# The third pair's rows in a buffer of their own, loaded between words; the first word operations behind the second pair's Exp

## The chip, the cores and the metric

One core of a Trainium2 chip runs the whole program. The metric is device time in microseconds for one execution. Engines are named as in the profile: PE is TensorE, DVE VectorE, ACT ScalarE, POOL GpSimd, SP SyncE.

## The reference

Attention with RMS-normalised q and k over 4 batches of 12 heads (448 positions, 64 features), and then two MLPs on 1792 tokens of 768 features:

```python
def rmsnorm(x, g):
    rms = np.sqrt(np.mean(x * x, axis=-1, keepdims=True) + 1e-06)
    return x / rms * g
q_n, k_n = rmsnorm(q, g_q), rmsnorm(k, g_k)
scores = np.matmul(q_n, k_n.transpose(0, 1, 3, 2)) / np.sqrt(64)
attn = softmax(scores)            # over the last axis
x = concat_heads(attn @ v)        # 1792 x 768
h = x @ w_in                      # 768 x 2048
x = np.maximum(0.01 * h, h) @ w_out
a, b = x @ w1, x @ w2             # 768 x 1024 each
out = ((a * b) @ w3) @ w_out2     # 1024 x 1024, 1024 x 768
```

Weights are 64-bit numbers; q, k and v are float32.

## The kernel before

The last two products have nothing between them, so the kernel multiplies their weights together first (w3 with w_out2, which it calls w_last; `combine_weights`, TensorE's line L554 with tile `pw`), during the first heads of the attention. The rest is the attention itself, two heads (a pair) at a time, and the MLPs, for which every product is made of float32 parts, a high one and a low one: a row of three matmuls (high by high, high by low, low by high).

A weight tile that comes as 64-bit numbers is loaded as **words** (768 KB for a tile of w_last, 512 KB for one of w3) and turned into float32 (`raw`) by four steps, written `to_float32`: ScalarE works on the high words in place (L470) and VectorE shifts them into raw (L472); ScalarE works on the low words in place (L474) and VectorE adds them to raw (L476). Then the parts: for w_last, GpSimd makes lasth (L110) and lastl (L199); for w3, ScalarE makes wh (L505) and VectorE wl (L199). The first four tiles of w_last and the first of w3 (t from 0 to 4 in the list of weights) are asked for at the start through SyncE's queue; later ones through ScalarE's, each behind an operation of ScalarE on earlier words (`self.rounded`).

A **pair** t of heads takes this way: `load_rows(t)` loads q and k with a position's features in a row (two DMAs, `qk_sb`, L139), two buffers for all pairs in turn; `statistics(t)` squares them (ScalarE, L153), sums (VectorE, L154), takes ScalarE's Ln (L157) and Exp (L158) for 1 / rms, refines it by a Newton step of five small operations (L160 to L164, on GpSimd but for the first pair), and scales k (VectorE, L174: kn). `keys(t)` transposes kn (TensorE, `pk`, L220) and splits it in kh (ScalarE, L229) and kl (VectorE, L230); `scores` multiplies with qh and ql (TensorE, `ps`, L128), VectorE scales (`p`, L265) and ScalarE takes the Exp (L274); `p_transpose` turns p (TensorE, `pt`) for `values`, which multiplies with v (`load_v`).

Pairs 0 and 1 are loaded by name at the start, pair 2's rows and statistics in step 0 of the list of attention steps. A scheduler with a model of time puts each engine's instructions in one order, by priorities and by `issue_after` (an instruction, or a DMA, doesn't stand ahead of the given one). At run time each engine and each DMA queue goes through its own order, waiting at whatever isn't ready. The queues' completions are counted on eight **lanes**, dealt out in turn; a DMA that gets a lane waits until the lane's DMA before has landed.

## Time and profile before

| what | value |
| --- | --- |
| time of the kernel, median of 3 runs | 1178.95 us (1178.59 to 1179.77) |
| the profiled execution's own time | 1182.5 us |
| its span, first to last instruction | 1180.7 us |
| TensorE busy | 1137.4 us, 96% of the span |
| VectorE, ScalarE, GpSimd busy | 710.1, 657.7, 243.6 us |
| mean granted clock of TensorE | 0.987 of full |

The runs' times count the whole program on the device; the span is that of one profiled execution, and lies 1.8 us below that execution's own time. TensorE is busy nearly all the time, so the views that tell something are those of the stretches in which it isn't.

### The profile page before, as it was taken

To read this page: it belongs to the slowest core of one execution; us is meant where nothing else is said; L and a number is where in the kernel's file an instruction comes from. 1 tells how busy PE (TensorE), PEld (TensorE's weight loads), DVE (VectorE), ACT (ScalarE), POOL (GpSimd) and SP (SyncE) were. 2 spreads that over 40 slices of the span, in tenths; PEclk is the share of its full clock that TensorE was granted. 3 is DMA by queue.
4 is the path that set the end of the run, shared out by engine and by line. 5 is a ranking of instruction groups with operands and counts; after the bars stand their busy time and mean duration, and the time that the engine had idled before them with its cause. 6 is when DMAs were issued, how large, how long until landed. Compare 5 with 4: busy or idle time off the path is not lost.

```text
span 1180.7 us, 16739 instructions
## 1 busy us (share of the span) xinstructions
PE 1137.4 (96%) x6096; PEld 956.8 (81%) x6096; DVE 710.1 (60%) x1334; ACT 657.7 (56%) x1347; POOL 243.6 (21%) x345
## 2 busy tenths in 40 slices
PE   3899999999999999999999999999999999899998
PEld 2678867677787888888888888879999999699997
DVE  7986776877423667567545643483445556954553
ACT  6978687987534566676556643354443344443331
POOL 5632344544212232345222011000000000000000
PEclk8799999999999999999999999999999999999999
DMA  9556565985865446346332421440212212102112
GB/s 315 182 176 221 174 204 193 326 279 186 292 209 162 153 139 206 127 138 200 123 120 95 161 87 43 143 151 28 81 51 57 69 41 78 55 29 89 55 36 103
DMA packets 74979, 164.51 MB, mean 139 GB/s; under 512 B 13968, under 2 KB 42384, under 8 KB 74896
## 3 DMA queue, kind: packets, MB, share of 16 engines
q1 hardware_dynamic: 55392, 80.06, 22.5%
q10 hardware_dynamic: 10800, 48.76, 12.3%
q0 software_dynamic: 8704, 34.61, 7.8%
q8 instruction: 48, 0.79, 0.3%
q14 instruction: 35, 0.29, 0.1%
HBM read 120.46 MB, written 42.95 MB: 138 GB/s over the span
## 4 chain that ended last, share of the span: by engine, by line
PE 84%; DVE 7%; ACT 4%; DMA 3%; issue 1%; ACTq 0%; SPq 0%; POOL 0%; DVEq 0%; POOLq 0%
PE ps_mm L554 32%; PE ps_o L554 13%; PE ps_b L554 9%; PE pt L308 6%; PE ps L128 6%; PE po L128 6%; PE ps_c L554 5%; PE pw L554 5%; PE ps_a L554 2%; DVE ol L199 1%; DMA wh<-kept_first_mlp_h 1%; ACT p L274 1%; DVE wl L199 1%; PE pk L220 1%; ACT w L474 1%
## 5 line engine op out<-in xcount | busy, mean ns | idle before, releaser
L199 DVE TENSOR_TENSOR wl<-raw,wh 128x512 fp32r<-128x512 f32 (+1 forms) x136 | 109.4, 807 | 112.4 <-ACT wh L505 73.5
L265 DVE TENSOR_SCALAR_CACHE_REDUCE p<-ps,rs 112x448 f32<-112x448 f32 x192 | 122.2, 680 | 42.4 <-PE ps L128 42.4
L554 PE MATMUL ps_mm<-xl,wh 128*128 128x448 f32 x384 | 146.2, 381 | 0.0
L554 PE MATMUL ps_mm<-xh,wh 128*128 128x448 f32 x384 | 141.3, 368 | 2.3 <-DMA wh<-kept_first_mlp_h 2.3
L274 ACT ACTIVATE p<-p,low 112x448 f32<-112x448 f32 x192 | 126.5, 662 | 30.1 <-DVE p L265 29.8
L554 PE MATMUL ps_mm<-xh,wl 128*128 128x448 f32 x384 | 141.5, 368 | 0.7 <-DMA wl<-kept_first_mlp_l 0.7
L554 PE MATMUL ps_mm<-gl,wh 128*128 128x448 f32 x288 | 109.5, 381 | 0.0
L554 PE MATMUL ps_mm<-gh,wl 128*128 128x448 f32 x288 | 105.6, 367 | 1.6 <-DMA wl<-kept_first_mlp_l 1.6
L554 PE MATMUL ps_mm<-gh,wh 128*128 128x448 f32 x288 | 106.0, 369 | 1.1 <-DMA wh<-kept_first_mlp_h 1.0
L554 PE MATMUL ps_o<-gl,wh 128*128 128x448 f32 x288 | 104.3, 366 | 0.0
L554 PE MATMUL ps_o<-gh,wl 128*128 128x448 f32 x288 | 100.8, 366 | 0.0
L308 PEld LDWEIGHTS pt<-ident,p 112*112 112x112 f32 x768 | 82.2, 136 | 21.3 <-issue 7.1
L554 PE MATMUL ps_o<-gh,wh 128*128 128x448 f32 x288 | 99.4, 366 | 0.0
L470 ACT ACTIVATE w<-w 128x768 f32<-128x768 f32 (+1 forms) x80 | 63.4, 792 | 64.6 <-DMA w<-w_out 29.7
L308 PE MATMUL pt<-ident,p 112*112 112x112 f32 x768 | 96.2, 265 | 0.0
L505 ACT ACTIVATE wh<-raw 128x512 fp32r<-128x512 f32 (+1 forms) x84 | 59.2, 706 | 56.5 <-PE ps_mm L554 52.6
L554 PEld LDWEIGHTS ps_mm<-xl,wh 128*128 128x128 f32 x384 | 72.4, 189 | 12.5 <-issue 7.2
L476 DVE CUSTOM_DVE_ANT_0 raw<-w,raw 128x1024 uint16<-128x1024 uint16 (+1 forms) x80 | 79.2, 995 | 2.2 <-ACT w L474 0.5
L554 PEld LDWEIGHTS ps_mm<-xh,wh 128*128 128x128 f32 x384 | 72.3, 188 | 9.4 <-issue 3.7
L784 ACT ACTIVATE wh<-raw 128x512 fp32r<-128x512 f32 (+1 forms) x52 | 36.3, 698 | 76.3 <-PE ps_b L554 33.7
L554 PEld LDWEIGHTS ps_mm<-xh,wl 128*128 128x128 f32 x384 | 72.6, 189 | 7.6 <-issue 1.6
L128 PE MATMUL po<-pth,v_sb 112*64 112x448 f32 x384 | 77.5, 545 | 0.0
(141 smaller groups left out, 2530.5 us busy)
## 6 DMA issues: line engine op xcount, KB each, us to landing
w<-w_in ACTq DMA_DIRECT2D x16, 768.0 KB, 5.8
w<-w_out ACTq DMA_DIRECT2D x24, 512.0 KB, 3.9
w<-w ACTq DMA_DIRECT2D x16, 768.0 KB, 4.5
qk_sb<-qk SPq DMA_DIRECT2D x48, 224.0 KB, 4.0
w<-w3t ACTq DMA_DIRECT2D x15, 512.0 KB, 4.6
kept_first_mlp<-raw POOLq DMA_DIRECT2D x16, 384.0 KB, 4.3
kept_first_mlp<-raw POOLq DMA_DIRECT2D x24, 256.0 KB, 3.2
kept_second_mlp<-raw POOLq DMA_DIRECT2D x16, 384.0 KB, 2.9
```

The lines of the kernel that those rows point to most:

```text
L128: one = nc.tensor.matmul(out, a, x, start=begin, stop=end)
L199: e.tensor_tensor(out, x, y.bitcast(F32), op=ALU.subtract)
L220: nc.tensor.transpose(pk[:, c * CP : (c + 1) * CP], kn[:, c].rearrange("p h d -> p (h d)"), ident[:CP, :CP],)
L265: nc.vector.tensor_scalar(p, ps[c % 2][e], x["scale"][:, e, c : c + 1], None, op0=ALU.mult, op1=ALU.min, accum_out=low,)
L274: exps[t] = nc.scalar.activation(p, p, AF.Exp, bias=low, scale=-1.0, accum_out=x["sums"][:, e, c : c + 1])
L308: nc.tensor.transpose(pt[:, c * CP : (c + 1) * CP], h["p"][c][:, kc * CP : (kc + 1) * CP], ident[:CP, :CP],)
L470: nc.scalar.activation(h, h, AF.Prelu, scale=2.0**-112, alpha=2.0**32)
L474: self.rounded = nc.scalar.activation(low, low, AF.Copy, scale=2.0**-29)
L476: nc.vector.tensor_tensor(top, top, low, op=ALU.add)
L505: self.rounded = nc.scalar.activation(flat[0], x, AF.Copy)
L554: nc.tensor.matmul(ps[:, :n], a, x, start=begin, stop=end, skip_group_check=on)
L784: nc.scalar.activation(parts[0], x, AF.Copy)
```

## The change

Pair 2's rows get a pool `extra` of one buffer, so their load needn't wait for pair 0's buffer. They are asked for in `Weights.load` directly behind the words of tile 1, and the first v behind those of tile 3. The words of tiles 2 and 3 stand behind the last load issued up to there (`start["dma"]`) in place of the second pair's `qt`. Step 0 of the attention no longer asks for v or rows; pair 3 takes pair 0's buffer. ScalarE's operations on the words of tiles 0 to 4 stand behind the Exp of pair 1's 1 / rms (`start["words"]`); before, those of tiles 0 and 1 stood behind kh of pair 0 (`start["keys"]`), and the others behind nothing.

```diff
+    extra = early_words.enter_context(tc.tile_pool(name="extra", bufs=1, side="right"))
...
         b, j = divmod(2 * t, H)
-        x = pairs[t]["rows"] = io.tile([CP, 2, 2, NCH, D], F32, tag="qk", name="qk_sb", bufs=2)
+        if t == 2:
+            x = extra.tile([CP, 2, 2, NCH, D], F32, name="qk_sb")
+        else:
+            x = io.tile([CP, 2, 2, NCH, D], F32, tag="qk", name="qk_sb", bufs=2)
+        pairs[t]["rows"] = x
...
-        nc.scalar.activation(rs, y, AF.Exp, scale=-0.5)
+        start["roots"] = nc.scalar.activation(rs, y, AF.Exp, scale=-0.5)
...
                 else:
-                    load_v(2 * t)
                     ranked(prep, t + 1)
-                    load_rows(t + STATS_AHEAD)
+                    if t:
+                        load_v(2 * t)
+                        load_rows(t + STATS_AHEAD)
...
-            with tc.issue_after((self.rounded or start["ins"]).ins):
-                eng.dma_start(x[:, :n], src.rearrange("p (n t) -> p n t", t=2))
+            behind = self.rounded or start["dma" if t in (2, 3) else "ins"]
+            with tc.issue_after(behind.ins):
+                dma = eng.dma_start(x[:, :n], src.rearrange("p (n t) -> p n t", t=2))
+            with tc.issue_after(dma.ins):
+                if t == 1:
+                    load_rows(2)
+                elif t == 3:
+                    load_v(0)
...
-            with tc.issue_after(start["keys"].ins) if t < 2 else ExitStack():
+            with tc.issue_after(start["words"].ins) if t <= KH2 else ExitStack():
                 nc.scalar.activation(h, h, AF.Prelu, scale=2.0**-112, alpha=2.0**32)
...
+    start["words"] = start["roots"]
```

KH2 is 4. The line numbers of the changed kernel are higher by up to 13. How the order moves, at three places. Numbers behind names tell buffers apart; the changed kernel's are a little higher (pair 2's rows are qk_sb_292 before and qk_sb_299 after).

ScalarE, around the squares of pair 2's rows, before. What stands in brackets is what the instruction waits for, DMAHW followed by a digit being a lane:

```order
L153 ACTIVATE sq_370<-qk_sb_292 112x512 [waits DMAHW0_49]
L153 ACTIVATE qk_sb_292<-qk_sb_292 112x512 [waits DMAHW1_49]
L451 DMA w64_467<-w_last 128x1536 [waits DVE_49]
L451 DMA w64_478<-w_last 128x1536 [waits DVE_49]
L470 ACTIVATE w64_356<-w64_356 128x768 [waits DMAHW2_49]
L474 ACTIVATE w64_356<-w64_356 128x768
L505 ACTIVATE wh_480<-raw_473 128x512 [waits DVE_49]
L451 DMA w3_487<-w3t 128x1024
```

And in the changed kernel:

```order
L158 ACTIVATE sq_373<-qk_sb_299 112x512 [waits DMAHW2_49]
L158 ACTIVATE qk_sb_299<-qk_sb_299 112x512
L458 DMA w64_470<-w_last 128x1536 [waits DMAHW2_49,DVE_49]
L482 ACTIVATE w3_389<-w3_389 128x512 [waits DMAHW4_49]
L486 ACTIVATE w3_389<-w3_389 128x512
L458 DMA w64_481<-w_last 128x1536 [waits DVE_49]
L517 ACTIVATE wh_483<-raw_476 128x512 [waits DVE_49]
L458 DMA w3_490<-w3t 128x1024 [waits DMAHW5_49]
L458 DMA w3_561<-w3t 128x1024 [waits DMAHW6_49]
L107 ACTIVATE pth_395<-pt_396 112x448 [waits PE_49]
L482 ACTIVATE w64_359<-w64_359 128x768
L486 ACTIVATE w64_359<-w64_359 128x768
```

The fifth tile of w_last (w64_356 before, w64_359 now) has gone from ahead of wh to behind it and an eviction (pth); the second w3 tile's two steps stand ahead of wh in its place. The issue of w64_470 now waits for lane 2, which is the lane of pair 2's rows and, in turn, of the first half of pair 3's rows (qk_sb_503), the next DMA that SyncE puts on it.

VectorE, from the first p of pair 1's scores on, before:

```order
L265 TENSOR_SCALAR p_448,low_449<-ps_432,rs_142 112x448
L472 TENSOR_SCALAR raw_492<-w64_356 128x768
L265 TENSOR_SCALAR p_452,low_453<-ps_433,rs_142 112x448
L199 TENSOR_TENSOR wl_481<-raw_473,wh_480 128x512
L476 ISA raw_492<-w64_356,raw_492 128x1536
L472 TENSOR_SCALAR raw_529<-w3_386 128x512
L265 TENSOR_SCALAR p_456,low_457<-ps_434,rs_142 112x448
L265 TENSOR_SCALAR p_460,low_461<-ps_435,rs_142 112x448
L476 ISA raw_529<-w3_386,raw_529 128x1024
```

And in the changed kernel:

```order
L270 TENSOR_SCALAR p_451,low_452<-ps_435,rs_145 112x448
L270 TENSOR_SCALAR p_455,low_456<-ps_436,rs_145 112x448
L204 TENSOR_TENSOR wl_484<-raw_476,wh_483 128x512
L484 TENSOR_SCALAR raw_495<-w64_359 128x768
L484 TENSOR_SCALAR raw_532<-w3_389 128x512
L270 TENSOR_SCALAR p_459,low_460<-ps_437,rs_145 112x448
L270 TENSOR_SCALAR p_463,low_464<-ps_438,rs_145 112x448
L488 ISA raw_495<-w64_359,raw_495 128x1536
L488 ISA raw_532<-w3_389,raw_532 128x1024
```

The fifth w_last tile's second step (to raw_492 before, raw_495 now) has gone from behind wl to behind wl, both first steps and two p.

GpSimd, from the fourth tile's lastl on, before:

```order
L199 TENSOR_TENSOR lastl_156<-raw_429,lasth_155 128x768
L110 TENSOR_SCALAR lasth_155<-raw_492 128x768
L160 TENSOR_SCALAR ss_369<-ss_369 112x16
L199 TENSOR_TENSOR lastl_156<-raw_492,lasth_155 128x768
L161 TENSOR_TENSOR y_376<-rs_375 112x16
L162 TENSOR_TENSOR y_376<-y_376,ss_369 112x16
L163 TENSOR_SCALAR y_376<-y_376 112x16
L110 TENSOR_SCALAR lasth_155<-raw_579 128x768
L164 TENSOR_TENSOR rs_375<-y_376,rs_375 112x16
L199 TENSOR_TENSOR lastl_156<-raw_579,lasth_155 128x768
```

And in the changed kernel:

```order
L204 TENSOR_TENSOR lastl_159<-raw_432,lasth_158 128x768
L165 TENSOR_SCALAR ss_372<-ss_372 112x16
L111 TENSOR_SCALAR lasth_158<-raw_495 128x768
L204 TENSOR_TENSOR lastl_159<-raw_495,lasth_158 128x768
L166 TENSOR_TENSOR y_379<-rs_378 112x16
L167 TENSOR_TENSOR y_379<-y_379,ss_372 112x16
L168 TENSOR_SCALAR y_379<-y_379 112x16
L111 TENSOR_SCALAR lasth_158<-raw_582 128x768
L169 TENSOR_TENSOR rs_378<-y_379,rs_378 112x16
L204 TENSOR_TENSOR lastl_159<-raw_582,lasth_158 128x768
```

The first Newton operation of pair 2 (ss) now stands ahead of the fifth tile's lasth; the others stand behind its lastl as before. For pair 1, further up, all five stand together, where lasth and lastl of the first tile stood between them.

SyncE's queue: before, v, words 0, 4, 1, a qt, words 2 and 3, a v, a qt, pair 2's rows, pair 3's rows; now words 0, 4, 1, the first half of pair 2's rows, a qt, their second half, words 2 and 3, a qt, both v, pair 3's rows, pair 4's rows.

## Rows read from the trace of the kernel before

**Rows 1.** The page's head and its first part: busy time of TensorE.

```profile
span 1180.7 us, 16739 instructions
...
PE 1137.4 (96%) x6096; PEld 956.8 (81%) x6096; DVE 710.1 (60%) x1334; ACT 657.7 (56%) x1347; POOL 243.6 (21%) x345
```

**Rows 2.** Waits of TensorE from 0 to 120 us: total, times, longest.

```profile
PE pk L220 <- DVE qk_sb L174: 9.3, 1, 9.3
PE pk L220 <- ACT p L274: 5.8, 1, 5.8
PE ps L128 <- DVE kl L230: 3.8, 1, 3.8
PE pw L554 <- DVE wl L199: 2.2, 1, 2.2
PE pw L554 <- ACT wh L505: 1.9, 2, 1.6
```

**Rows 3.** Two windows: busy us and count of PE, PEld, DVE, ACT, POOL; clock, DMA share, GB/s.

```profile
25.00:30.00 5.00, 1.76 (x8) 0.83 (x8) 5.00 (x4) 1.60 (x5) 4.92 (x4) 0.82 1.06 320
50.00:55.00 5.00, 5.00 (x30) 4.25 (x29) 5.00 (x8) 5.00 (x12) 3.93 (x4) 0.93 0.00 0
```

**Rows 4.** Timeline of ScalarE, 10 to 50 us: start, duration, instruction, [idle before <-releaser].

```profile
25.82 0.19 ACT L274 ACTIVATION_READ_ACCUMULATOR p<-p,low 112x1 f32 x1
29.06 0.60 ACT L153 ACTIVATE sq<-qk_sb 112x512 f32<-112x512 f32 x1 [3.06 <-DMA qk_sb<-qk]
30.02 0.63 ACT L153 ACTIVATE qk_sb<-qk_sb 112x512 f32<-112x512 f32 x1 [0.36 <-DMA qk_sb<-qk]
...
30.89 0.92 ACT L470 ACTIVATE w<-w 128x768 f32<-128x768 f32 x1 [0.24 <-DVE r L284]
...
32.52 0.62 ACT L505 ACTIVATE wh<-raw 128x512 fp32r<-128x512 f32 x1
...
40.12 0.20 ACT L158 ACTIVATE rs<-y 112x16 f32<-112x16 f32 x1
```

**Rows 5.** Timeline of VectorE, 10 to 50 us, same columns.

```profile
20.75 0.69 DVE L174 TENSOR_TENSOR qk_sb<-qk_sb,rs 112x512 f32<-112x512 f32 x1
...
25.78 4.09 DVE L476 CUSTOM_DVE_ANT_0 raw<-w,raw 128x1536 uint16<-128x1536 uint16 x2
29.79 0.67 DVE L230 SCALAR_TENSOR_TENSOR kl<-pk,gqk,kh 128x448 fp32r<-128x448 f32 x1
...
34.70 0.95 DVE L476 CUSTOM_DVE_ANT_0 raw<-w,raw 128x1536 uint16<-128x1536 uint16 x1
35.56 0.42 DVE L472 TENSOR_SCALAR raw<-w 128x512 uint32<-128x512 uint32 x1
35.90 0.68 DVE L265 TENSOR_SCALAR_CACHE_REDUCE p<-ps,rs 112x448 f32<-112x448 f32 x1
...
37.11 2.32 DVE L476 CUSTOM_DVE_ANT_0 raw<-w,raw 128x1024 uint16<-128x1024 uint16 x1
...
43.90 2.32 DVE L174 TENSOR_TENSOR qk_sb<-qk_sb,rs 112x512 f32<-112x512 f32 x1 [1.67 <-POOL rs L164]
46.14 0.68 DVE L199 TENSOR_TENSOR wl<-raw,wh 128x512 fp32r<-128x512 f32 x1
```

**Rows 6.** Timeline of GpSimd, 10 to 50 us, same columns.

```profile
35.74 0.94 POOL L110 TENSOR_SCALAR lasth<-raw 128x768 fp32r<-128x768 f32 x1 [3.25 <-DVE raw L476]
...
37.03 1.84 POOL L199 TENSOR_TENSOR lastl<-raw,lasth 128x768 fp32r<-128x768 f32 x1
40.41 1.90 POOL L161 TENSOR_TENSOR y<-rs 112x16 f32<-112x16 f32 x1 [1.53 <-ACT rs L158]
42.38 0.22 POOL L162 TENSOR_TENSOR y<-y,ss 112x16 f32<-112x16 f32 x1
...
43.84 1.83 POOL L199 TENSOR_TENSOR lastl<-raw,lasth 128x768 fp32r<-128x768 f32 x1
```

**Rows 7.** The page's part 6: DMA issues, KB each, median us to landing.

```profile
qk_sb<-qk SPq DMA_DIRECT2D x48, 224.0 KB, 4.0
```

More of the change, by code (lines that the diff above doesn't have):

```diff
@@ L472, in to_float32 @@
             nc.vector.tensor_scalar(top, high, 3, None, op0=ALU.logical_shift_left)
-            with tc.issue_after(start["keys"].ins) if t < 2 else ExitStack():
+            with tc.issue_after(start["words"].ins) if t <= KH2 else ExitStack():
                 self.rounded = nc.scalar.activation(low, low, AF.Copy, scale=2.0**-29)
```

## The prediction

> **What bounds the kernel now.** First the page's head: TensorE is busy for 1137.4 of 1180.7 us [rows 1]. A gain is a stall of TensorE that goes; a loss is one that grows. Next, where those stalls are, by TensorE's waits in the first 120 us: 9.3, 5.8, 3.8, 2.2 and 1.9 us in five rows, 23.0 us together, over half of the 43.3 that the span has [rows 1, 2]. They end with the wait for wl, which VectorE delivers at 46.14 + 0.68 = 46.82 [rows 5]. In the window from 50 us on TensorE is busy for 5.00 of 5 [rows 3]. So one instant sums up the start: when this second wl (of the second w3 tile) is there. What is gained earlier and not still there at 46.8 is waited away again; what is lost there moves all that follows.
>
> Who sets that instant? Read the three elementwise engines' timelines backwards from it. wl stands on VectorE right behind kn of the third pair, which waited 1.67 us for GpSimd's rs and then took 2.32 us, against 0.69 for the same instruction at 20.75 [rows 5]. It ran beside a lastl of 1.83 us [rows 6]. That rs is the fifth Newton step, whose second began at 40.41 after 1.53 us of waiting for ScalarE's Exp, at 40.12 [rows 4, 6]. Further up, ScalarE stood idle 3.06 + 0.36 = 3.42 us for the third pair's rows for the halves that it uses at 29.06 and 30.02 [rows 4]. VectorE has no such gap: it is busy 5.00 of 5 where ScalarE is busy 1.60 [rows 3].
>
> **Step 1: the rows in their own buffer, loaded between words.** They are asked for before two of the w_last tiles, so the 3.42 us in front of the squares go. What is late next? In the new order the issue of a w_last tile (w64_470) comes two places behind, on the squares' own lane. The lane's next user is the first half of the fourth pair's rows, which now stands where the third pair's stood: behind all words. Ahead of it SyncE has the same transfers as before and 448 KB more, the third pair's two halves of 224 KB [rows 7]. At the 320 GB/s of that window [rows 3] these are 1.4 us, so it lands between 29.06 (as the half before it did) and 30.5; I take the middle, 29.8. ScalarE is through with its squares at 25.82 + 0.19 + 0.60 + 0.63 = 27.2 [rows 4] and would stand 2.6 us at the issue: three quarters of the wait has moved on by two instructions. Behind it queue two conversion steps and wh. The two steps from 30.89 to 32.52 cost 1.63 for a w_last tile [rows 4]; the w3 tile that stands here now has two thirds of its columns, 1.1. wh then begins at 29.8 + 1.1 = 30.9, 1.6 us ahead of 32.52 (0.9 to 2.3 by the bounds). The w_last tile that now stands ahead of wh, from 30.89, comes behind it and one eviction, so not before 30.9 + 0.62 = 31.5 [rows 4]: that tile is not ahead.
>
> A transfer's share of the engines is the weak point of that 29.8. The Trainium skill, DMA: Bandwidth & Descriptors, section "Queues, rings and completion order", has each DMA engine take turns among the queues that have work for it. By that rule SyncE's transfers move faster as long as ScalarE has issued none, and ScalarE's first issues come later in the changed order, so the lane would be free sooner than a count of bytes says. No row of this trace separates the two queues' rates; what follows from an early lane is the first rival below.
>
> **Step 2: words let go behind the second pair's Exp.** Squares, Ln and Exp now come ahead of all words, and the five Newton steps are together on GpSimd. Kn of that pair, at 20.75 now [rows 5], comes some us earlier. Yet its scores need kl at 29.79, and kl stands behind a pair of conversions that take 4.09 us [rows 5]; VectorE is full, and the conversions ahead of kl are the same five tiles in both orders. That cover makes the step worth 0. The bounds: 0.7 us later (ScalarE waits for VectorE's sums before any word, a gap about as long as one 0.67 us instruction) to 0.7 earlier (kn no longer ahead of the conversions). Were the cover gone, it would be worth the 5.8 us that TensorE waits ahead of those keys [rows 2].
>
> **Step 3: the fifth w_last tile falls back on VectorE.** Now its second step (to raw_492) starts at 34.70 directly behind wl. In the new order the w3 tile's first step and two p stand between. By the spacing of the rows: 35.90 - 35.56 = 0.34 for the step, and for two p, which fill the time from 35.90 to the next step, 37.11 - 35.90 = 1.21 [rows 5]. That is 1.55 us. The tile's lasth and lastl follow on GpSimd, now from 35.74 and until 37.03 + 1.84 = 38.87 [rows 6]. With 1.55 they end at 40.4, and if the next conversion on VectorE (0.68 without company, an estimate from kl's row of 0.67, since its own row, 2.32, holds its wait beside lastl [rows 5]) gets in before them, at 41.1. The Newton steps of the third pair, of which the first now stands ahead of that lasth, begin at 40.41 today, held by ScalarE's Exp and not by GpSimd. With GpSimd free only at 41.1 they start 0.7 later.
>
> Then comes what can't be read off: which collisions the steps meet. A small one of them took 1.90 us at 40.41, where its neighbours take about 0.2 [rows 6]: 1.7 us for one collision. Nothing makes it more or less likely in the new order except that the conversions beside it sit 1.55 later; I put a quarter, 0.4 us, on a further one. Kn's own 2.32 stays, since in the new order too a lastl follows right behind the rs that lets kn go. Lower bound of the step: 0 (Exp still last, GpSimd done in time, ScalarE's 1.6 from step 1 pulling all of it forward). Upper bound: lasth and lastl wholly between Exp and Newton steps, 0.94 + 1.84 = 2.8 [rows 6].
>
> Of collisions the Trainium skill, SBUF — State Buffer, section "SBUF: two separate sides", says that VectorE and GpSimd share a port pair as a lock for the whole of an instruction. By it the engine that comes second pays the other's full time, so an order that is hardly different can give or take a lastl. The rows of kn and lastl agree: kn, 43.90 to 46.22, ends about half a us behind a lastl that ends at 43.84 + 1.83 = 45.67 [rows 5, 6].
>
> **The sum.** Step 1: 0 by itself, since its 1.6 us come ahead of the instant, the tile that leads to wl has none of them, and they are in step 3's lower bound. Step 2: 0. Step 3: 0.7 + 0.4 = +1.1. wl is there at 47.9 in place of 46.82. Moving v behind the words costs nothing: v is used by the first values, two pairs later. The loads of later pairs' rows are asked for earlier than they are needed either way. Behind 50 us the order of every engine is the same but for a few rows, so the 1.1 is carried to the end. The profiled execution took 1182.5 and would take 1183.6; the median of the runs is 3.55 below the profiled one, 1178.95 + 1.1 = 1180.0.
>
> **Rivals.**
> *Faster: the lane is free in time.* If the fourth pair's half lands before 27.2, ScalarE's 3.42 us go for good, wh, the w_last tile, Exp and kn all move by them, and wl is there at 43.4. TensorE has the stalls to take it: 1.9 for wh and 2.2 for wl are 4.1 [rows 2]. That gives 1175.5. For it: ScalarE's own transfers start later, leaving SyncE's more of the engines. Against: VectorE is full through that stretch and must keep up as well. It decides from a tile's second step that ends before 34.9.
> *Slower: GpSimd's lasth and lastl push the Newton steps out.* One mechanism, at GpSimd between 36 and 42: if lasth starts behind about 39, both stand wholly behind the Exp, and the price is the 2.8 above: 1181.8. For it: 1.55 us of delay are in the order itself and the lane's wait keeps ScalarE from making up for it. Against: lasth has 3.4 us to fall back from 35.74.
> *Nothing changes.* Exp remains last, as at 40.12; rows and words come in other order but wl stays at 46.8 within half a us: 1179.0. For it: VectorE is the full engine, and its work is the same.
>
> **How the numbers follow.** Forecast (+1.1) 0.37, nothing changes 0.20, faster 0.21, slower 0.22. A measurement of this kernel can tell about 0.2%, 2.36 us, from no change: below 1176.6 or above 1181.3. The first two lie inside: 0.57, of which 0.03 go to slower for the forecast's upper side and 0.01 come back from the faster case when half of it arrives: faster 0.20, same 0.55, slower 0.25. The range takes the slower rival with another half a collision (1181.8 + 0.9) on top, 1182.7, and on the low side the greater part of the faster one, 1175.9. The likeliest case's own range is 1178.3 to 1181.8, by step 2's 0.7 below no change and step 3's upper bound.
>
> **What would show each step right or wrong.** Step 1: no wait of ScalarE ahead of the third pair's squares, but one of some 2.6 us behind them with a transfer of rows as its end; wrong if ScalarE runs through. Step 2: kn of the second pair well ahead of 20.75, kl still near 29.8. Step 3: lasth of the fifth tile past 37, the Newton steps behind its lastl, wl at about 47.9. The prediction is wrong if TensorE's last long wait of the start ends before 45 or after 50, or if a stall that isn't in the trace now shows up behind 60 us.

## The result, and the profile after

The changed kernel takes 1187.38 us (median of 6 runs, 1184.56 to 1188.77) against 1180.09 for the kernel before in the same comparison (6 runs, 1178.59 to 1184.51): a ratio of 1.0059, 95% interval 1.0038 to 1.0080. It is slower, by more than the range allowed. The prediction had started from 1178.95, the median of three runs of the kernel before; six give 1180.09, so 1.1 of the 7.4 us between forecast and result lie in the kernel before itself. The changed kernel's profiled execution took 1187.14 us with a span of 1185.3. The page's head:

```profile
span 1185.3 us, 16739 instructions
...
PE 1140.8 (96%) x6096; PEld 958.8 (81%) x6096; DVE 712.3 (60%) x1334; ACT 657.8 (55%) x1347; POOL 241.8 (20%) x345
```

The span has grown by 4.6 us over [rows 1]. TensorE is busy for 3.4 of them and idle for the rest: the loss is partly stalls and partly the same matmuls at a lower clock. TensorE's waits from 0 to 120 us (total, times, longest):

```profile
PE pk L225 <- DVE qk_sb L179: 9.1, 1, 9.1
PE ps L129 <- DVE kl L235: 4.5, 1, 4.5
PE pw L566 <- ACT wh L517: 3.1, 1, 3.1
PE ps L129 <- ACT kh L234: 2.9, 2, 2.2
...
PE pt L313 <- DVE rb L363: 0.9, 1, 0.9
PE pw L566 <- DVE wl L204: 0.3, 1, 0.3
```

Against [rows 2] three things matter. The wait for wl is almost gone (2.2 before), the one for wh has grown from 1.9 to 3.1, and there is one for rb, the product of the first pair's values with 1 / sums (`x` in the values' end), that before has nowhere. The instants around them, in TensorE's timeline (start, duration, instruction, idle before and its releaser):

```profile
44.13 0.69 PE L566 MATMUL pw<-lasth,wh 128*128 128x384 f32 x1 [3.06 <-ACT wh L517]
...
48.27 0.69 PE L566 MATMUL pw<-lasth,wl 128*128 128x384 f32 x1 [0.32 <-DVE wl L204]
...
65.40 0.98 PE L313 MATMUL pt<-ident,p 112*112 112x112 f32 x8 [0.89 <-DVE rb L363]
...
179.39 0.45 PE L129 MATMUL ps<-kh,qh 64*112 64x448 f32 x1 [1.15 <-DVE rb L363]
```

The last one is a second rb, that of the sixth pair's values, at 178 us: the prediction looked nowhere near it. In the kernel before, TensorE's wait for the same wh (the second) ended at 42.20, and the two rb stood on VectorE at 60.50 and 174.12, the second ahead of kn of the ninth pair:

```profile
42.20 0.45 PE L554 MATMUL pw<-lasth,wh 128*128 128x384 f32 x1 [1.58 <-ACT wh L505]
```

```profile
60.50 0.62 DVE L358 TENSOR_TENSOR rb<-po,rb 128x448 f32<-128x448 f32 x1
...
174.12 0.61 DVE L358 TENSOR_TENSOR rb<-po,rb 128x448 f32<-128x448 f32 x1
...
177.11 0.69 DVE L174 TENSOR_TENSOR qk_sb<-qk_sb,rs 112x512 f32<-112x512 f32 x1 [1.25 <-POOL rs L164]
```

In the changed kernel, ScalarE's timeline, against [rows 4]:

```profile
26.83 0.57 ACT L158 ACTIVATE sq<-qk_sb 112x512 f32<-112x512 f32 x1
27.35 0.61 ACT L158 ACTIVATE qk_sb<-qk_sb 112x512 f32<-112x512 f32 x1
31.38 0.33 ACTq L458 DMA_DIRECT2D w<-w_last  x1
31.76 0.67 ACT L482 ACTIVATE w<-w 128x512 f32<-128x512 f32 x1 [3.80 <-DVE raw L488]
...
40.80 0.24 ACT L163 ACTIVATE rs<-y 112x16 f32<-112x16 f32 x1
```

No wait stands ahead of the squares now; one of 3.80 us stands behind them. The row names VectorE, yet the DMA issue at 31.38 was queued ahead, and the transfer records have the first half of pair 3's rows, the lane's user, landing at 31.30, 0.08 us ahead of that issue. VectorE's timeline, against [rows 5]:

```profile
14.49 0.69 DVE L179 TENSOR_TENSOR qk_sb<-qk_sb,rs 112x512 f32<-112x512 f32 x1 [0.66 <-POOL rs L169]
...
27.43 4.08 DVE L488 CUSTOM_DVE_ANT_0 raw<-w,raw 128x1536 uint16<-128x1536 uint16 x2
31.44 0.67 DVE L235 SCALAR_TENSOR_TENSOR kl<-pk,gqk,kh 128x448 fp32r<-128x448 f32 x1
...
40.19 2.15 DVE L484 TENSOR_SCALAR raw<-w 128x768 uint32<-128x768 uint32 x1 [0.36 <-ACT w L482]
...
45.30 2.31 DVE L179 TENSOR_TENSOR qk_sb<-qk_sb,rs 112x512 f32<-112x512 f32 x1
47.53 0.68 DVE L204 TENSOR_TENSOR wl<-raw,wh 128x512 fp32r<-128x512 f32 x1
...
64.72 0.62 DVE L363 TENSOR_TENSOR rb<-po,rb 128x448 f32<-128x448 f32 x1
...
178.11 0.69 DVE L179 TENSOR_TENSOR qk_sb<-qk_sb,rs 112x512 f32<-112x512 f32 x1 [1.92 <-POOL rs L169]
178.72 0.62 DVE L363 TENSOR_TENSOR rb<-po,rb 128x448 f32<-128x448 f32 x1
```

Kn of the second pair comes 6.3 us earlier, kl 1.65 later, and wl is there at 47.53 + 0.68 = 48.21, 1.39 behind 46.82. GpSimd's timeline, against [rows 6]:

```profile
38.78 1.22 POOL L111 TENSOR_SCALAR lasth<-raw 128x768 fp32r<-128x768 f32 x1 [1.56 <-DVE raw L488]
40.09 1.83 POOL L204 TENSOR_TENSOR lastl<-raw,lasth 128x768 fp32r<-128x768 f32 x1
41.88 0.53 POOL L166 TENSOR_TENSOR y<-rs 112x16 f32<-112x16 f32 x1
42.49 1.02 POOL L167 TENSOR_TENSOR y<-y,ss 112x16 f32<-112x16 f32 x1
```

The fifth tile's lasth and lastl now end at 41.92, behind the Exp (40.80 + 0.24), and the Newton steps begin at 41.88 in place of 40.41. Three windows (columns as in [rows 3]):

```profile
25.00:30.00 5.00, 2.02 (x8) 1.08 (x8) 4.89 (x5) 2.96 (x8) 3.85 (x3) 0.50 1.05 361
45.00:50.00 5.00, 4.68 (x17) 3.28 (x16) 4.71 (x6) 5.00 (x10) 2.07 (x3) 0.50 0.35 113
50.00:55.00 5.00, 5.00 (x20) 3.92 (x20) 5.00 (x9) 5.00 (x12) 2.94 (x3) 0.62 0.00 0
```

From 25 to 30 us the granted clock was 0.50, the lower of the two levels, where it was 0.82 before. From 45 to 50 it was 0.50 in the kernel before as well:

```profile
45.00:50.00 5.00, 3.12 (x10) 3.06 (x10) 4.91 (x10) 5.00 (x10) 1.02 (x2) 0.50 0.10 42
```

From 50 on it was 0.62 in place of 0.93: 20 matmuls in 5 us instead of 30. The wait for wl is so short because TensorE itself came to it late. Its wait for the second wh ended at 44.13 in place of 42.20, and the 13 matmuls from there to the end of the last one ahead of wl took 3.82 us at a clock of 0.50, where they had taken 2.51 at 0.82.

**Where the time goes.** Each kernel has the same 4272 matmuls of weights (L554 before, L566 after). I take the start of the k-th of them in both traces and subtract. The 36th is the first group behind the second wl (49.92 us before), the 101st starts at 71.01, the 201st at 100.65, the 401st at 179.70. One column is the difference at the 36th, the next three what each stretch adds, then the difference at the 401st, and last the ratio of all runs with its interval. All in us; one profiled execution each.

Two things in the columns are not loss. TensorE's first matmul, which waits for the first rows, starts at 9.29 us before, at 9.83 in e8 (the same kernel again) and at 8.94 to 9.52 in the changed kernel. Counted from it, the two executions of the kernel before agree to 0.01 us at the 36th matmul, and the changed kernel is 1.2 to 2.0 late there, 1.6 in the mean. And at the 101st TensorE has done eight transposes more than before in every kernel but e8 and e2 (0.98 us, the row at 65.40 above); the next column gives that back. So these two columns are best read together.

| kernel | 36th | to 101st | to 201st | to 401st | at 401st | ratio |
|---|---|---|---|---|---|---|
| changed | 1.39 | 1.69 | -0.81 | 1.34 | 3.61 | 1.0059 (1.0038 to 1.0080) |
| e1_after_again | 0.91 | 2.20 | -0.31 | 2.15 | 4.95 | 1.0051 (1.0037 to 1.0065) |
| e9_after_same_chip | 1.84 | 1.69 | -0.22 | 3.09 | 6.40 | 1.0047 (1.0033 to 1.0061) |
| e13_after_third | 1.63 | 1.67 | -0.54 | 4.18 | 6.94 | 1.0051 (1.0031 to 1.0072) |
| e17_after_fourth | 1.57 | 1.66 | -0.82 | 1.11 | 3.52 | 1.0042 (1.0021 to 1.0063) |
| e8_before_again | 0.53 | 0.20 | -0.02 | 0.11 | 0.82 | one run |
| e2_rows_only | 2.01 | -1.80 | -0.02 | 0.08 | 0.27 | 1.0020 (1.0005 to 1.0035) |
| e3_release_only | 2.39 | 1.63 | 0.74 | 0.52 | 5.28 | 1.0041 (1.0027 to 1.0056) |
| e4_lane_free | 4.35 | 0.28 | -0.94 | 0.80 | 4.49 | 1.0054 (1.0035 to 1.0074) |
| e5_rb_first | 2.78 | 0.32 | -0.61 | 1.32 | 3.81 | 1.0012 (0.9992 to 1.0032) |
| e6_fifth_first | 3.62 | -1.31 | 0.79 | 0.04 | 3.14 | 0.9995 (0.9971 to 1.0018) |
| e11_fifth_first_again | 3.31 | -1.38 | 0.56 | 0.36 | 2.85 | 1.0025 (1.0015 to 1.0034) |
| e12_both_first | 4.38 | -2.05 | 0.26 | 0.83 | 3.42 | 1.0021 (1.0005 to 1.0037) |
| e7_before_rb_late | -0.90 | 4.29 | -0.79 | 0.03 | 2.63 | 0.9995 (0.9971 to 1.0019) |
| e10_before_both_rb_late | 0.61 | 1.50 | -0.74 | 1.00 | 2.37 | 1.0002 (0.9988 to 1.0017) |
| e14_sixth_rb | 1.45 | 1.67 | -0.27 | 0.00 | 2.85 | 1.0045 (1.0025 to 1.0064) |
| e15_first_rb | 1.56 | 0.35 | -0.62 | 2.63 | 3.92 | 1.0041 (1.0021 to 1.0060) |
| e16_both_rb | 2.63 | 0.51 | -0.65 | 2.45 | 4.94 | 1.0024 (1.0006 to 1.0042) |
| e18_both_rb_again | 1.51 | 0.30 | -0.60 | 0.24 | 1.45 | 1.0030 (1.0008 to 1.0052) |

In the five executions of the changed kernel the parts average 1.47 + 1.78 - 0.54 + 2.37 = 5.08 us at the 401st matmul. From there to the end of the span they take 997.4 to 1002.0 us, the two of before 1001.0 and 996.9: behind 186 us nothing is lost that can be told from no change. So the loss is made in three places: the start, the stretch from 50 to 74 us, the stretch from 103 to 186 us.

### The profile page after: what moved, and what is told of

Same layout as the page of the kernel before. It is cut to its first block, busy times and chain, and to the rows that moved or that the text cites. A ratio compares the mean times of both kernels' runs of the same rounds, so it can differ in the third digit from the quotient of the medians.

```text
span 1185.3 us, 16739 instructions
## 1 busy us (share of the span) xinstructions
PE 1140.8 (96%) x6096; PEld 958.8 (81%) x6096; DVE 712.3 (60%) x1334; ACT 657.8 (55%) x1347; POOL 241.8 (20%) x345
## 4 chain that ended last, share of the span: by engine, by line
PE 71%; DVE 5%; ACT 4%; DMA 4%; issue 1%; POOL 0%; ACTq 0%; SPq 0%; DVEq 0%; POOLq 0%
PE ps_mm L566 29%; PE ps_o L566 13%; PE ps_b L566 10%; PE ps_c L566 5%; PE po L129 4%; PE pt L313 4%; PE ps L129 4%; PE ps_a L566 2%; DVE ol L204 1%; ACT p L279 1%; DMA wh<-kept_first_mlp_h 1%; DMA w<-w_in 1%; DMA w<-w 1%; DVE wl L204 1%; ACT w L486 1%
## 5 line engine op out<-in xcount | busy, mean ns | idle before, releaser
L566 PE MATMUL ps_mm<-xl,wh 128*128 128x448 f32 x384 | 145.9, 380 | 0.8 <-POOL xl L204 0.8
L270 DVE TENSOR_SCALAR_CACHE_REDUCE p<-ps,rs 112x448 f32<-112x448 f32 x192 | 121.9, 679 | 41.1 <-PE ps L129 41.1
L279 ACT ACTIVATE p<-p,low 112x448 f32<-112x448 f32 x192 | 126.5, 662 | 30.5 <-DVE p L270 30.4
L566 PE MATMUL ps_mm<-xh,wl 128*128 128x448 f32 x384 | 141.3, 368 | 1.9 <-DMA wl<-kept_first_mlp_l 1.9
L566 PE MATMUL ps_mm<-xh,wh 128*128 128x448 f32 x384 | 141.1, 368 | 0.6 <-DMA wh<-kept_first_mlp_h 0.6
L566 PE MATMUL ps_mm<-gl,wh 128*128 128x448 f32 x288 | 110.1, 383 | 0.0
L566 PE MATMUL ps_mm<-gh,wl 128*128 128x448 f32 x288 | 106.5, 370 | 1.8 <-DMA wl<-kept_first_mlp_l 1.8
L566 PE MATMUL ps_mm<-gh,wh 128*128 128x448 f32 x288 | 106.8, 372 | 0.5 <-DMA wh<-kept_first_mlp_h 0.5
L566 PE MATMUL ps_o<-gl,wh 128*128 128x448 f32 x288 | 104.2, 366 | 0.0
L482 ACT ACTIVATE w<-w 128x512 f32<-128x512 f32 (+1 forms) x80 | 64.1, 801 | 69.8 <-DMA w<-w_out 27.9
L566 PE MATMUL ps_o<-gh,wl 128*128 128x448 f32 x288 | 100.6, 366 | 0.0
L566 PE MATMUL ps_o<-gh,wh 128*128 128x448 f32 x288 | 99.3, 366 | 0.0
L566 PEld LDWEIGHTS ps_mm<-xl,wh 128*128 128x128 f32 x384 | 72.2, 188 | 13.4 <-issue 6.9
L566 PEld LDWEIGHTS ps_mm<-xh,wl 128*128 128x128 f32 x384 | 72.3, 188 | 8.8 <-DMA wl<-kept_first_mlp_l 2.2
L566 PEld LDWEIGHTS ps_mm<-xh,wh 128*128 128x128 f32 x384 | 72.1, 188 | 7.7 <-issue 2.0
```

Source lines behind the costliest of these rows:

```text
L270: nc.vector.tensor_scalar(p, ps[c % 2][e], x["scale"][:, e, c : c + 1], None, op0=ALU.mult, op1=ALU.min, accum_out=low,)
L279: exps[t] = nc.scalar.activation(p, p, AF.Exp, bias=low, scale=-1.0, accum_out=x["sums"][:, e, c : c + 1])
L482: nc.scalar.activation(h, h, AF.Prelu, scale=2.0**-112, alpha=2.0**32)
L566: nc.tensor.matmul(ps[:, :n], a, x, start=begin, stop=end, skip_group_check=on)
```

## The experiments

At first two theories stood against each other: that the words let go late (step 2) make everything on VectorE late (A), and that ScalarE's wait at the lane (step 1) does (B). When both parts alone had been seen, a third took their place: VectorE's order far behind the edit, where rb has moved (C). Its rival is that the loss is made up to 51 us and the wait for rb only shows it (D). All kernels compute the whole output.

**The changed kernel again, on other chips** (no edit): e1, e9, e13, e17.

> The changed kernel once more, as it is, to see which of its stalls come back. The profiled pair shows +1.0 us at the first pw, +1.4 at the wait for the second wl, +3.1 when the hundredth L566 matmul runs (71 us against 74 us), and then between +1.6 and +5.0 later on. If the loss is made in the first 71 us, that part comes back (+2.5 to +3.5 at the hundredth matmul) and the rest wanders by a us or two either way; the time is then 0.2 to 0.4% above before. If the order behind 71 us costs something by itself, the same places (178 us, 380 us) stall again and the time is 0.5% or more above before.

> The changed kernel on the chip of the next three, so that they can be set against it and not only against before, whose runs spread over 12 us on the chip of the last group. Expected 0.4 to 0.6% above before; TensorE's waits for rb at 64 us and at 178 us come back, 1 to 2 us each.

> The changed kernel beside the next three on one chip. Three looks so far put its 200th matmul 2.3 to 3.3 us and its 400th 3.6 to 6.4 us behind the profiled before; the same again, and 0.4 to 0.6% above before.

> The changed kernel, unaltered, once more beside the next one. If the two late products of the values (the first pair's and the sixth pair's) carry most of the loss, it stands 0.45 to 0.6% above the kernel before, with a TensorE wait of some 1.5 us at 65 to 67 us and the matmul products some 5 us late at 186 us. If the loss is chance between chips, it comes within 0.3%.

Measured: 1186.08, 1186.64, 1186.82 and 1185.42 us, with the ratios of the table. The loss is no accident of one chip. ScalarE's wait behind the squares was 4.42, 3.68 and 4.16 us in the first three, and each trace puts it down to something else (r, raw, the rows): the lane's wait has no name of its own in this view. The transfer records have it: in all five executions the issue starts 0.07 to 0.08 us behind the landing of the first half of pair 3's rows, which comes at 31.30 to 32.08. e17 falls a little short of its expectation (0.42%, 3.52 us at the 401st matmul).

**Half of the change each.** rows_only is the changed kernel with before's release of the words:

```diff
-            with tc.issue_after(start["words"].ins) if t <= KH2 else ExitStack():
+            with tc.issue_after(start["keys"].ins) if t < 2 else ExitStack():
```

(at both of ScalarE's word steps); release_only is the kernel before with the opposite lines, and otherwise its own loads:

```diff
-            with tc.issue_after(start["keys"].ins) if t < 2 else ExitStack():
+            with tc.issue_after(start["words"].ins) if t <= KH2 else ExitStack():
...
+    start["words"] = start["roots"]
```

> Half of the change: the third pair's rows in their own buffer, loaded between words, v behind the words; ScalarE's first word operations released as before (behind kh of the first pair, tiles 0 and 1). Theory A, that the loss comes from VectorE's conversions beginning 2.4 us later (first step at 15.19 against 12.82), expects kl of the second pair back near 29.8 and a time within 0.2% of before. Theory B, that it comes from the wait which moved to the issue of a w_last tile on the lane of the fourth pair's rows, expects ScalarE to stand again until about 31.3, and a time 0.2 to 0.6% above before.

> The other half: ScalarE's operations on the first five word tiles behind the second pair's Exp; rows and v loaded as before. Theory A expects kl of the second pair near 31.4 and the whole loss, 0.3 to 0.6% above before. Theory B expects no loss, within 0.2%, since the third pair's rows keep their place and no lane is turned.

Measured: 1182.47 and 1184.86 us, before 1179.99 on that chip. Both halves cost, the release more. kl ends its wait at 31.58 in rows_only, as late as in the changed kernel (31.44), and that execution has lost only 0.27 us at the 401st matmul: a late kl is not what costs by then. (At 1180.97 us it is one of the faster of the twelve; what makes the median 1182.47 is not in it.) Rows_only has the same lane wait, 3.40 us, too. release_only has lost 5.28 there, and TensorE's wait for the keys is 4.9. B had expected no loss of it. The two halves also differ in the first rb, which runs at 59.87 in rows_only and, behind a wl and sums, at 66.47 in release_only (60.50 before).

**The lane set free.** Both loads of v moved behind the first store of 1 / sums, so that fewer transfers stand ahead of pair 3's rows, which are the former user of w64_470's lane here too:

```diff
-            nc.sync.dma_start(rd.rearrange("n (p c) -> p n c", c=NCH), r)
+            one = nc.sync.dma_start(rd.rearrange("n (p c) -> p n c", c=NCH), r)
+            if t == 0:
+                with tc.issue_after(one.ins):
+                    load_v(0)
+                    load_v(2)
```

> The whole change, but the first two v are asked for behind the first store of 1 / sums (some 15 us later), so that fewer transfers stand ahead of the fourth pair's rows and the w_last tile's issue waits on a lane that is free early. Theory B expects ScalarE to run through at 28 us and the loss to go, within 0.2% of before. Theory A expects ScalarE's wait to go and the time to stay as slow as the changed kernel, since wh and kl still wait for VectorE's conversions that end at about 31.5.

Measured: 1185.94 us, ratio 1.0054. The first half of pair 3's rows landed at 27.74, the issue went out at 27.82, and ScalarE's idle time behind the squares fell from 3.80 to 0.64 us, so the lane was the cause of that wait. The time did not fall, because a wait came out elsewhere (TensorE's waits, 0 to 75 us):

```profile
PE pw L569 <- DVE wl L204: 5.3, 1, 5.3
```

wl is there at 50.49 + 0.68 = 51.17, 2.96 us later than in the changed kernel, though the wh that it needs is earlier (42.63 for 43.44). The edit has moved GpSimd's order too: lasth and lastl of the sixth w_last tile now stand ahead of the third pair's Newton steps, whose second begins at 47.12 in place of 41.88, and kn stands ahead of wl:

```profile
49.26 1.30 DVE L179 TENSOR_TENSOR qk_sb<-qk_sb,rs 112x512 f32<-112x512 f32 x1 [0.40 <-POOL rs L169]
50.49 0.68 DVE L204 TENSOR_TENSOR wl<-raw,wh 128x512 fp32r<-128x512 f32 x1
```

So e4 shows the cause of ScalarE's wait. What that wait costs it does not show, since another order hides it.

**VectorE's order around the first rb.** The order of the compiled kernels, before and changed; rb is the row that starts with L358 and L363:

```
67 L472 TENSOR_SCALAR raw_846<-w3_567 128x512
68 L476 ISA raw_846<-w3_567,raw_846 128x1024
69 L358 TENSOR_TENSOR rb_347<-po_699,rb_347 128x448
70 L283 TENSOR_SCALAR r_618<-sum_431 112x8
```

```
67 L484 TENSOR_SCALAR raw_849<-w3_570 128x512
68 L488 ISA raw_849<-w3_570,raw_849 128x1024
69 L204 TENSOR_TENSOR wl_779<-raw_773,wh_778 128x512
70 L484 TENSOR_SCALAR raw_908<-w3_653 128x512
71 L204 TENSOR_TENSOR wl_838<-raw_790,wh_837 128x512
72 L488 ISA raw_908<-w3_653,raw_908 128x1024
73 L288 TENSOR_SCALAR r_621<-sum_434 112x8
74 L484 TENSOR_SCALAR raw_996<-w3_662 128x512
75 L363 TENSOR_TENSOR rb_350<-po_702,rb_350 128x448
```

Two wl, a conversion, two first steps and the small operation on the sums have gone ahead of rb. rb_first puts it ahead of the last of them by

```diff
+            with tc.issue_after(start["first_values"].ins) if t == 13 else ExitStack():
+                nc.vector.tensor_scalar(top, high, 3, None, op0=ALU.logical_shift_left)
...
+            with tc.issue_after(start["first_values"].ins) if t == 11 else ExitStack():
+                subtract("V" if own else "P", flat[1], x, flat[0])
```

(`start["first_values"]` is the first rb). fifth_first makes a later tile's first step wait for the fifth w_last tile's last step on VectorE, so that the latter stands ahead again (more has moved with it: the second wl now stands ahead of kn, five score matmuls ahead of the first matmul with wl, and the first rb behind one wl in place of two):

```diff
+            with tc.issue_after(start["fifth"].ins) if t == KH2 + 2 else ExitStack():
+                nc.vector.tensor_scalar(top, high, 3, None, op0=ALU.logical_shift_left)
...
+            one = nc.vector.tensor_tensor(top, top, low, op=ALU.add)
+            if t == KH2 + 1:
+                start["fifth"] = one
```

both_first has both edits. rb_late goes the other way: the kernel before, with its first rb (in `finish`) issued behind the wl of tile 12:

```diff
+            one = subtract("V" if own else "P", flat[1], x, flat[0])
+            if t == 12:
+                with tc.issue_after(one.ins), tc.high_priority(PRIORITY["values"]):
+                    start["finish"]()
```

> The changed kernel with one thing turned back on VectorE: the first values' product with 1 / sums (rb, L363 there) stands ahead of the second and third of three w3 tiles' steps and two wl again, as in the kernel before; nothing ahead of it moves. Theory C, that the part of the loss behind 51 us comes from rb standing too late there (TensorE waits for it at 64.5 us, 0.9 and 1.5 us in two runs), expects that wait gone, the hundredth matmul of L566 1 to 2 us after that of before (3.1 in the changed kernel), and a time 1 to 2 us below the changed kernel, some 0.35% above before. Theory D, that the loss is made up to 51 us alone (words later, TensorE at the low clock) and the wait only shows it, expects the hundredth matmul to stay 3 us late and the time as the changed kernel's, 0.5% above before.

> The changed kernel with the first values' rb ahead of the w3 tile's steps and wl, once more, now beside the changed kernel. Theory C expects the stretch from the second wl to the 200th matmul 1.5 to 2 us shorter than in the changed kernel and the time 1 to 2 us below it; the wait at 178 us stays.

> The changed kernel with the fifth w_last tile's conversion ahead of the second w3 tile's first step on VectorE, nearly as before. My step 3 expects lasth and lastl of that tile on GpSimd 0.5 to 1.5 us earlier than in the changed kernel (38.8 and 41.9), the second wl 0.5 to 1 us earlier than 48.2, and a time 0.5 to 1 us below the changed kernel. The rival, that the tile's place has no effect because the Newton steps wait for ScalarE's Exp (40.8) and for collisions, expects no difference that can be told.

> The changed kernel with the fifth w_last tile's conversion ahead of the second w3 tile's first step, once more beside the changed kernel itself. In the group before it showed no wait for rb at 178 us and a time as before's. If that belongs to it, it is 3 to 5 us faster than the changed kernel here; if it was that chip's spread, within 2 us of it.

> The changed kernel with both: the fifth w_last tile's conversion ahead, and the first values' rb ahead of the w3 tile's steps and wl. Theory C expects neither of TensorE's waits at 64 and 178 us, the 100th matmul within 1.5 us of before, and a time within 0.2% of before, 4 to 6 us below the changed kernel. If words that begin 2.4 us later are the loss by themselves (theory A), it stays 0.3% or more above before.

> The kernel before with one thing moved: the first values' product with 1 / sums (rb, L358) on VectorE behind the two wl and two sums that follow it, where the changed kernel has it; everything else keeps its order. Theory C expects TensorE to wait for it at 62 to 65 us, 1 to 2 us, and the time 0.1 to 0.2% above before. Theory D expects no wait (TensorE has other work, VectorE is as far as before) and a time within 0.1%.

Measured, in the traces: with rb at its old place (e5, e15) the stretch to the 101st matmul adds 0.3 us, with rb late 1.7 to 2.2 in the changed kernel. Up to the 201st, where both have done the same matmuls as before, it is -0.3 against 0.8 to 1.9. e5's 101st matmul is 3.1 us late all the same, as D expected, but 2.78 of that was there at the 36th. In the kernel before, making rb late brings a wait of TensorE that was not there, one step on, for the pth made from what rb's release lets through (its timeline, around 67 us, in e10, which has this edit too):

```profile
68.73 0.45 PE L128 MATMUL ps<-kh,qh 64*112 64x448 f32 x1 [1.46 <-ACT pth L106]
```

In e7 it is 1.51, and that stretch, which also had a clock of 0.89 from 60 to 75 us, adds 4.29. So the wait follows rb's place. Up to the 201st matmul e10 adds 0.76 (1.50 - 0.74) and e7, with the fallen clock, 3.50. In the total it is not to be seen alone: e7 0.9995, e10 (below) 1.0002, e5 1.0012, e15 1.0041, all with intervals of about 0.2% to each side, and 1.5 us are 0.13%. fifth_first came out at 0.9995 and then at 1.0025, both_first at 1.0021: better than the changed kernel (by 2.8 and 2.9 us on e9's chip, where C had expected 4 to 6 of both_first), in no case faster than before. In those three the 36th matmul is over 3 us late, but TensorE has then done 123 matmuls in place of 118 (as in e2 and e4), which is why the next stretch gives back 1.3 to 2.1. What step 3 expected of fifth_first did not come: lasth of the fifth tile starts at 39.06 in e6 and its lastl ends at 42.25, no earlier than 38.78 and 41.92, and wl is there 0.47 us earlier (47.74) because it no longer stands behind kn.

**The sixth pair's rb.** In the changed kernel kn of the ninth pair, which waits 1.92 us for GpSimd's rs, stands directly ahead of it (the rows at 178 us above); before, it stood three rows behind. sixth_rb swaps these two neighbours and nothing else:

```diff
+        if t == 5:
+            with tc.issue_after(one.ins), tc.high_priority(PRIORITY["statistics"]):
+                start.pop("ninth")()
```

(`one` is the rb, `start["ninth"]` the kn). e10 is the kernel before with both rb late, the first as in e7 and the second by

```diff
+            with tc.issue_after(start["kn8"].ins) if t == 5 else ExitStack():
+                nc.vector.tensor_tensor(x, po[:, :S], x, op=ALU.mult)
```

(`kn8` is kn of the ninth pair). both_rb is the changed kernel with the edits of rb_first and sixth_rb. e8 is the kernel before, unaltered.

> The changed kernel with two neighbours on VectorE changed over and no other row moved: the sixth values' rb ahead of the ninth pair's kn (which waits for GpSimd), as before has it. Theory C expects TensorE's wait for rb at 178 us (1.2 to 1.8 us) gone, the stretch between the 200th and 400th matmul 1 to 2.5 us shorter than the changed kernel's, and the time 1 to 2.5 us below it. The rival, that the wait only shows a lateness which comes from elsewhere, expects the stretch and the time unchanged.

> The kernel before with two instructions moved on VectorE and nothing else: the first values' rb behind the two wl (as in the group before), and the sixth values' rb behind the ninth pair's kn, where the changed kernel has it. Theory C, that these two places make the loss, expects a wait of TensorE for each (1 to 2 us at 67 and at 176 us), the 200th matmul 2 to 3 us and the 400th 3 to 4.5 us late, and a time near the changed kernel's, 0.3 to 0.5% above before. If the second place costs nothing without the rest of the change (TensorE has other rows to run), the 400th stays 2 to 3 us late.

> The changed kernel with both of these. Theory C expects what is left of the loss to be that of the start, 1.1 us as forecast, with the 400th matmul 1 to 2 us behind before and the time within 0.2% of before (0.1% above). If the time stays 0.3% or more above before, the two places are not the loss.

> Both products of the values are back at their old places on VectorE. If they carry most of the loss, it stands 0.15 to 0.3% above the kernel before, at least 2 us below the changed kernel by the medians of this chip, without a wait near 65 or 179 us. If the start alone carries it (wl late), it stands where the changed kernel does, within 1 us.

> The kernel before, one more look at its stages: which of its stalls behind 180 us (306, 310, 377, 379, 1011, 1019 us, and TensorE at 0.91 of full clock from 300 to 320) come back. If those wander, what the profiled pair shows behind 180 us is chance, and only the part up to 180 us (+3.6 and +4.9 in two looks at the changed kernel) belongs to the change; the hundredth matmul comes at 71.0 within 0.3 us in either case.

TensorE's waits from 60 to 190 us in e14:

```profile
PE pt L320 <- DVE rb L370: 1.5, 1, 1.5
PE pk L232 <- DVE qk_sb L181: 1.5, 1, 1.5
```

and in e17, the changed kernel:

```profile
PE pt L313 <- DVE rb L363: 1.5, 1, 1.5
PE pk L225 <- DVE qk_sb L179: 1.5, 1, 1.5
PE ps L129 <- DVE rb L363: 1.0, 1, 1.0
```

The swap removes the third row and leaves the first; the stretch to the 401st matmul adds 0.00 in place of 1.1 to 4.2. The second row is there in the kernel before as well (1.5 us). Where the clock doesn't fall, the stretch adds about what TensorE waits for this rb: 1.34 for a wait of 1.15 in the changed kernel, 2.15 for 1.79 in e1, 1.11 for 1.0 in e17, 1.32 for 1.14 in e5, 0.80 for 0.70 in e4, 0.52 for 0.41 in e3, 0.36 for 0.27 in e11, and 0.08 and 0.04 for none in e2 and e6. But the wait is not the whole of that stretch. It is 1.15, 1.79, 1.49 and 1.0 us in four executions of the changed kernel and missing in e13, where the most was lost. 1.3 of that came at 123 us, with a wait of 0.94 us for a pth that no other execution of this kernel has. For the rest the clock fell instead (windows of e13, then of e16, which has no late rb):

```profile
174.00:178.00 4.00, 4.00 (x14) 1.45 (x16) 2.25 (x8) 4.00 (x12) 1.13 (x1) 0.58 0.31 91
178.00:182.00 4.00, 4.00 (x32) 2.46 (x28) 2.09 (x4) 0.82 (x3) 1.06 (x5) 0.99 0.44 111
```

```profile
174.00:178.00 4.00, 4.00 (x18) 1.52 (x15) 2.90 (x6) 2.82 (x8) 0.38 (x2) 0.69 0.54 163
```

Four us at 0.58 are 1.7 us of matmuls lost. It happened in e9, e13, e15 and e16, directly behind the wait for qk_sb at 170 us in three and behind that for rb at 179 in e9, and in neither trace of the kernel before, which has the wait for qk_sb too. Nor does it hang on the sixth rb, since e16 has it and e18, the same kernel, has not. Nor does the late place alone bring the wait. e10 has the late sixth rb and no wait at 178: there TensorE had other matmuls ahead of the scores that wait. e2, e6, e12 and e15 have it late and don't wait either (e15, which was expected to, had the fallen clock). So the wait takes the place on VectorE, TensorE's own order and a TensorE that is not late itself.

Totals: e14 1184.72, e15 1183.22, e16 1182.33 us, beside 1186.82 for the changed kernel on the same chip, before 1180.49. With both rb back, six of the twelve runs are below the fastest of the nine of the changed kernel (1182.28). On the next chip the pair was 1184.01 (e18) against 1185.42 (e17), before 1181.04. Both times the repair is nearer to before, by 4.5 and by 1.4 us, the second of them within the noise (1.0030 against 1.0042, and their intervals overlap by most of their width). The direction repeats, the size does not, and neither gets back to before. Two expectations of C failed here: the 401st matmul of e16 was to be 1 to 2 us late and is 4.94, of which 2.63 were there at the 36th and the fallen clock made much of the rest, and e18 was to be at least 2 us below the changed kernel.

## Why the prediction was wrong, step by step

**Step 1, the lane: right in mechanism.** ScalarE runs through its squares, 26.83 and 27.35, and then stands at the issue, 3.80 us in place of 2.6, since pair 3's half landed at 31.30 and not at 29.8 (the upper bound was 30.5). e4 shows that it is the lane. With it the wh that was to begin at 30.9, 1.6 us early, began at 32.90, 0.4 late.

The worth of 0 at the end held only by a margin. Ten executions have the changed kernel's order up to 50 us (the five of that kernel, e5, e14, e15, e16, e18), and in them the lane's transfer lands anywhere from 30.88 to 33.21. The second wh begins 12.0 to 12.2 us behind the issue in all ten. Counted from TensorE's first matmul, the second wl ends at 38.9 to 39.1 where the issue comes by 22.9, and 16.3 behind the issue where it comes later (23.0 to 24.2: e1, e13, e5, e16). In the profiled execution the issue came at 22.31, so about half a us was left; what lands later than that is paid in full, as in e5 and e16, whose 36th matmul is 2.6 to 2.8 us late.

The prediction had weighed the rule on taking turns among queues (the Trainium skill, DMA: Bandwidth & Descriptors, section "Queues, rings and completion order"), from which an earlier landing would have followed. The half landed 1.5 us behind the middle that the count of bytes gave, with 361 GB/s moved in that window, so it was not early; no run separates the queues' shares.

**Step 2, the words: the cover held, the size was off.** Kn came early (14.49) and gained nothing, as put. kl was to stay near 29.8 within 0.7; it began at 31.44, since the pair of conversions ahead of it starts at 27.43 in place of 25.78 (VectorE's first step on words had started at 15.19 in place of 12.82). That it is as late in rows_only says that this is not the release of the words alone, and rows_only's 0.27 us at the 401st matmul that by itself it cost nothing further.

**Step 3, the fifth tile: right on VectorE and GpSimd, near in size, in part by luck at TensorE.** lasth at 38.78 is past 37, lastl ends at 41.92 (41.1 put), the Newton steps stand behind it with a collision of 1.02 in the second one, kn takes 2.31. wl is there at 48.21 where 47.9 was put: +1.39 for +1.1. By the start alone the median would have been 1178.95 + 1.4 = 1180.3, inside the range. One reading was wrong: that the second wl sums up the start. TensorE waits 0.32 us for it, since its wait for the second wh ended 1.93 us later and it went on at a clock of 0.50. In e1 and e13 it does not wait for wl at all, and the 36th matmul is late by 0.91 and 1.63 even so. That the start cost about what was put is in part luck.

**The failed step** is the sentence "Behind 50 us the order of every engine is the same but for a few rows, so the 1.1 is carried to the end." Two of those few rows are rb. The first one, six rows down, makes TensorE wait 0.9 to 1.5 us at 64 to 66 us; putting it back took 1.3 to 1.5 us out of that stretch's 1.78 in four traces (e5, e15, e16, e18). The second, behind a neighbour that waits, makes it wait 1.0 to 1.8 us at 178; swapping the two took it out (e14, e16, e18). With 1.47 for the start, 1.4 for the first and 1.1 for the second (the mean over the five executions, 0 in e13) they make 4.0 of the 5.08 us at the 401st matmul; the runs' medians differ by 4.4 to 7.3 us in the five comparisons. The term that the prediction put at nothing, what the moved rows cost behind 50 us, is thus the larger part of the loss. The prediction had named such a stall behind 60 us as what would make it wrong; it did not search the order for one, though the order shows both moves.

The rivals: the lane was not free in time, so the faster one is out. The slower one (Newton behind lasth and lastl) is about half true: the steps stand behind the lastl, but by 1.47 us, not by 2.8. None of the rivals had a loss behind 50 us.

**What stays open.** Why the clock falls near 175 us in some executions and not in others, and so how much of the loss from 103 to 186 us the change itself makes. How much of the total each rb carries: the traces show each wait come and go, the totals tell the two together from nothing on one chip of two, and not one from the other. Making both late in the kernel before did not move its total (1.0002, 0.9988 to 1.0017); its trace loses 0.76 us to the first and does not wait for the second, and so little lies within that interval. Executions scatter (the kernel before took 1175.38 to 1184.81 on the last chip), and a stall of one us can be given back or doubled later.

## What to carry to other kernels

Where a scheduler sets the order, an edit at the start moves rows far behind it: list for the whole program the instructions that another engine waits for, here the products that let the next transposes or scores go, and price each that has moved against what now stands ahead of it, above all a neighbour that itself waits. Two executions agree in a stall and not in what it costs at the end, so read the place from the trace by comparing the start of the same k-th matmul in both kernels (counted from the first matmul, and at a k where both have done the same other matmuls), and the size only from repeated totals on one chip.

## What the runs showed of the hardware that was not expected

A DMA issue that waits for its lane stops ScalarE's operations queued behind it without being named: the same wait of 3.4 to 4.4 us was put down to raw, r, ss and qk_sb in four traces. The issue starts 0.07 to 0.08 us behind the landing that it waits for in the five executions of the changed kernel and in e4, where that landing came at 27.74 and the idle time was 0.64 us.

A stretch at the lower clock can hide a stall and cost about the same. In the changed kernel's first profile TensorE waits 0.89 us for rb, with a clock of 0.81 over 50 to 60 us; in its four repeats, with 0.87 to 0.99 there, it waits 1.5. The stretch adds 1.69 there and 1.66 to 2.20 here. The same at 178 us: with the clock at 0.58 ahead of it the wait for rb was gone and the loss was larger.

VectorE and GpSimd can delay each other by most of an instruction: the first step on a w_last tile took 2.15 us beside a lastl from 40.09 to 41.92, where the same form at 15.19 and 17.74 took 0.57 and 0.56. The Trainium skill, SBUF — State Buffer, section "SBUF: two separate sides", describes such a lock, and this trace agrees.
